# Second-level products for M7 and a new order of M6 and M7 in the last pass of a fused linear-attention and SwiGLU kernel

## The chip, the cores and the metric

The kernel runs on one core of one Trainium2 chip. The metric is the device time of one execution in microseconds. Three runs of the kernel before gave 756.44 us in the median (755.99 to 761.65). The profile is one more execution of the same program, recorded by the hardware profiler.

Names of engines as in the profile: PE is TensorE (matmuls), PEld its weight loads, DVE is VectorE, ACT is ScalarE, POOL is GpSimd, SP is SyncE, which here only issues DMAs. An engine name with a q (SPq, POOLq) is the engine's sequencer.

## The reference

The input is a sequence of 2048 rows of 1024 in bfloat16. What is computed, cut to the part that matters:

```python
def reference(A_x, A_wqkv, A_wo, B_x, B_w_gate, B_w_up, B_w_down):
    x = A_x
    xn = _layernorm(x, axis=-1)
    s = _A_ref(xn, A_wqkv, A_wo)          # linear attention, 32 heads of 32
    g = _silu(_B_ref(xn, B_w_gate, B_w_up, B_w_down))
    return x + s * g

def _B_ref(x, w_gate, w_up, w_down):      # w_gate, w_up: 1024 x 3584, w_down: 3584 x 1024
    g = _silu(x @ w_gate)
    u = x @ w_up
    return (g * u) @ w_down
```

## The kernel before

**Stages.** The first third of the time computes the attention part and stores `s` in DRAM. Then come two passes over 1024 tokens each, and each pass has two stages: a loop of 28 iterations (14 groups of gate columns and 14 of up columns, "keys") that makes the hidden activations `h`, and a down stage that multiplies `h` by `w_down`, applies silu, multiplies by `s` and adds `x`. The change touches the last pass alone: its loop (lines 1693 to 1744) and its down stage, `emit_down_m` (line 1394).

**Seven products in place of eight.** All large products use the scheme of Strassen and Winograd: a matrix product is cut into 2 x 2 quadrants and made of seven half-size products of sums of quadrants, so TensorE does 7/8 of the work and the other engines make the sums. In `emit_down_m` the seven are called M1 to M7. With `A` the activations, the operands on their side are A11 for M1, A12 for M2, A22 for M4 and the sums S1 = A21 + A22 (for M5), S2 = S1 - A11 (M6), S3 = A11 - A21 (M7) and S4 = A12 - S2 (M3). S1, S2 and S4 are written over A21, A11 and A12; S3 has two buffers of its own (`s3_`). The same sums of the weights are made in advance, in the first pass or earlier, and lie in DRAM (`wd_drams`).

**The second level.** The products listed in `L2` (M1, M2 and M4) are cut once more: `l2_M` (line 1469) makes each of seven quarter-size products, numbered 1 to 7 and taken in the order of `L2_ORDER`, 1, 2, 5, 6, 7, 4, 3. Each is made for two row halves r by `l2_p`, seven matmuls of 256 columns for each half. A product that is not in `L2` is made by `prod_t` in four tiles t of 128 rows, 14 matmuls of 512 columns each. The second level needs sums on both sides:

- of the weights: `l2_load` (line 1102) loads two blocks of a packed weight into a slot, `l2_sums` (line 1134) makes four differences on POOL and issues the store of the seven operands to DRAM on POOL's queue. One such load, sum and store is called a unit. M1 and M4 have four units each, in the loop of the last pass; M2's are made in the first pass.
- of the activations: `l2_lhs` (line 1160) makes four sums for one of seven blocks j on POOL, into the buffers of `l2_bufs`: for M1 two weight slots (`r_spare`), for M2 and M4 two tiles left from the first pass (`x_spare`, "kept" in the profile).

**Weight slots.** `w_slot` gives a tile from a pool of eight. Weights come through `load_w` in the order of `w_seq`; `load_w_to(n)` asks for all up to the n-th. In the loop iteration i calls `load_w_to(base + i + 5)`, from 17 on `+ 6`. Staged units take their slots from the same pool, and from iterations 17 and 18 on two more are set apart for `r_spare`. In the down stage `load(M, q)` asks for weights six or eight ahead; a product at the second level has four loads (three of 896 KB and one of 448), another has two halves of four DMAs each (line 260).

**Order of the work.** A manual schedule (line 382) keeps PE, DVE, ACT and POOL in the order of the program text. SP is not in it here: its order is made by the framework's planner, and like every queue it then runs in that order, so that a DMA that waits holds those behind it.

**One second-level product.** `l2_M` has two pairs of PSUM banks, `xw` and `zy`, each bank in two halves of 256 columns (`lo`, `hi`). Products 1 and 2 go to xw lo, 5 and 3 to xw hi, 6 to zy hi, 7 and 4 to zy lo; ACT copies between them, and the results are taken out by ACT (M1) or DVE additions, which all go through the helper `tt` (line 1418). For M1, whose results go straight to `KA`, these lines stand ahead of product 3, which writes `xw` hi again:

```python
for r in range(2):
    c0, c1 = c[r]
    ...
    tt(c1[:, hi], xw[r][:, hi], c1[:, hi])
fill()
```

`fill` inserts work for PE: in M1 the first two products of M2, in M2 the first tile of the next M. `banks` hands out two sets of four PSUM banks in turn. `sums` makes S1, S2 or S4 in seven operations of 1024 elements. `fins` and `flush` hold and run the final steps (`fin`, line 1196): two DVE operations (lines 1200, 1201), an out DMA and `io_load`, the load of the next x and s rows into one of five buffers.

Of the kernel before, what the change touches and what calls it, by code (L numbers as in the profile page):

```python
# [10 lines left out]
ALU = mybir.AluOpType  # L11
# [10 lines left out]
def kernel(  # L22
# [11 lines left out]
    nc = tc.nc  # L34
# [30 lines left out]
    NPK = 8  # L65
# [121 lines left out]
    NPASS = NB // 2  # L187
    passes = list(range(NPASS - 1, -1, -1))
    NWA = NFG // 2
    M_ORDER = (1, 2, 7, 6, 5, 4, 3)  # L190
    L2 = (1, 2, 4)
    L2_ORDER = (1, 2, 5, 6, 7, 4, 3)
    NQ = NFG // 2
    CH = CW // 2
    l2_drams = {}
# [756 lines left out]
    with ExitStack() as p3:  # L952
# [145 lines left out]

        l2_q = deque((M, j) for M in L2 if M != 2 for j in range(0, NQ, 2))
        l2_live = deque()  # L1100

        def l2_load():
            M, j0 = l2_q.popleft()
            kd, q = M_PACK[M]
            t = w_slot()
            v = t[:].rearrange("p h a b -> p (h a b)").rearrange("p (b j n) -> p b j n", b=8, n=CH)
            js = range(j0, min(j0 + 2, NQ))
            for j in js:
                for k, b0, b1 in ((0, 0, 7), (1, 1, 6)):
                    src = wd_drams[j][0 if kd == "a" else 1][:, k, q].rearrange("p (c n) -> p c n", n=CH)  # L1110
                    nc.sync.dma_start(out=v[:, b0:b1 + 1:b1 - b0, j - j0, :], in_=src)
            l2_live.append((M, js, v))
# [34 lines left out]
        x_spare, r_spare = [], []  # L1147

        def l2_bufs(M):
            v = [x[:].rearrange("p a b -> p (a b)").bitcast(F16) for x in x_spare]  # L1150
            if M == 1:
# [4 lines left out]
        def l2_quad(A, j):  # L1156
            v = A[:, :, j].rearrange("p k (r t n) -> p k r t n", r=2, t=2)
            return v[:, 0, :, 0], v[:, 1, :, 0], v[:, 0, :, 1], v[:, 1, :, 1]

        def l2_lhs(M, A, j, eng):  # L1160
            a11, a12, a21, a22 = l2_quad(A, j)
# [13 lines left out]
        for p in passes:  # L1175
# [4 lines left out]
            for hf in (1, 0):  # L1180
                for t in (2 * hf, 2 * hf + 1):
                    fq += [(p, t + TPB, 0), (p, t, 1), (p, t, 0)]

        def io_load(after=None):
            if not fq:
                return
            p, t, cc = key = fq.pop(0)
            r0 = p * TB2 + t * P
            pool, tg = (sp, "S%d" % len(fq)) if len(fq) < 3 else (iop, "io")
            io = pool.tile([P, 2, CW], BF16, name="io", tag=tg)  # L1190
            gate([nc.sync.dma_start(out=io[:, 0, :], in_=x2[r0:r0 + P, cc * CW:(cc + 1) * CW]),
                  nc.sync.dma_start(out=io[:, 1, :], in_=s_dram[r0:r0 + P, cc * CW:(cc + 1) * CW])],
                 after, sync=True)
            io_tiles[key] = io
# [199 lines left out]
        def emit_down_m(p, h, base):  # L1394
# [8 lines left out]
            def load(M, q=None):  # L1403

                n_ = max(i for i, key in enumerate(seq) if key[2][0] == M and q in (None, key[2][1])) + 1
                load_w_to(base + n_ + (NPK - 2 if M == 1 and q != 3 else NPK))

            def S3(k):
                return s3_[k // NWA][:, k % NWA]

            def lhs_of(M):
                if M == 7:
                    return S3
                v = {1: A11, 2: A12, 3: S4, 4: A22, 5: S1, 6: S2}[M]
                return lambda k: v[:, k]

# [52 lines left out]
            def l2_M(M, A, K, done, fill, in_place, dst=None):  # L1469
# [17 lines left out]
                load(M, 1)  # L1487
                for r in range(2):
                    l2_p(M, 7, r, A, bk)
                if K is None:  # L1490
# [19 lines left out]
                for r in range(2):  # L1510
                    c0, c1 = c[r]
                    if K is None:
                        nc.scalar.copy(out=c1[:, lo], in_=zy[r][:, lo])
                    else:
                        tt(c1[:, lo], zy[r][:, lo], K[2 * r + 1][:, lo])
                        done(2 * r + 1, c1)
                    l2_p(M, 3, r, A, bk)
                    if in_place:
# [17 lines left out]

            load_w_to(base + NPK - 2)
            KA = kept("kA")
            fins = deque()
            M7, M6, M5 = [], [], []  # L1540
            KB = []

            def fill7():
                M7.extend(banks())
                KB.extend(kept("kB"))
                prod_t(7, 0, M7[0], True)

            def done2(t, c):
                fins.append((t, 0, silu(c, "g11")))
            m2 = l2_M(2, quads(h, 1, 0), KA, done2, fill7, False)  # L1550
            for k in range(NFG):
                tt(S3(k), A11[:, k], A21[:, k], ALU.subtract)
            go(l2_M(1, quads(h, 0, 0), None, None, lambda: next(m2), False, KA))
            sums(S1, A21, A22, ALU.add)
            go(m2)
            sums(S2, S1, A11, ALU.subtract)
            for t in range(TPB):
                if t:
                    prod_t(7, t, M7[t], True)
                tt(KB[t], M7[t], KA[t])  # L1560
                flush(1)
            load(7)
            sums(S4, A12, S2, ALU.subtract)
            for j in range(NQ):
                l2_lhs(4, quads(h, 1, 1), j, nc.gpsimd)
            M6 = banks()
            for t in range(TPB):
                prod_t(6, t, M6[t], True)
                tt(KB[t], M6[t], KB[t])
                tt(KA[t], M6[t], KA[t])  # L1570
# [43 lines left out]
        for pi, p in enumerate(passes):  # L1614
# [78 lines left out]
            for i in range(n):  # L1693
                if first:
                    load_w_to(base + i + (na0 if i < n - 7 else 8 if i > n - 6 else 7))
                else:
                    load_w_to(base + i + (5 if i < 17 else 6))
                if i + 1 < n:
                    emit_a(keys[i + 1])
                    emit_c22(keys[i + 1])  # L1700
# [31 lines left out]
                if not first:  # L1732
                    if l2_live:
                        l2_sums()
                    if i in (17, 18):
                        r_spare.append(w_slot())
                    if i % 2 == 1 and l2_q:
                        l2_load()
                    if i >= 18 and 4 * l2_j + 4 <= i:
                        l2_lhs(1, quads(h, 0, 0), l2_j, nc.gpsimd)  # L1740
                        l2_lhs(2, quads(h, 1, 0), l2_j, nc.gpsimd)
                        l2_j += 1
                if deferred:
                    deferred.pop(0)()
            base += n
            if last_pass:
                l2_lhs(2, quads(h, 1, 0), NQ - 1, nc.gpsimd)
# [36 lines left out]
```

## Time and profile before

| | us |
|---|---|
| median of three runs (lowest, highest) | 756.44 (755.99, 761.65) |
| the profiled execution | 756.18 |
| its span, first to last instruction | 754.4 |
| the last pass: loop, down stage | 499 to 669, 669 to 754 |

Granted TensorE clock: 0.999 of full speed. Times in the trace count from the start of the span. A group line of the page gives line, engine, operation, output and input tiles, shape and count, then busy time, mean of one in ns, and idle time of the engine just before. Matmul lengths are modelled and overlap: 512 columns appear as 379 ns each, while in the stream they start 216 ns apart.

Busy time by engine in some stretches of the last pass (columns: stretch, its length, then PE, PEld, DVE, ACT and POOL busy with counts, clock, share of the DMA engines, GB/s):

```profile
539.00:560.00 21.00, 21.00 (x99) 9.47 (x97) 14.36 (x17) 7.08 (x10) 6.14 (x7) 1.00 0.80 274
640.00:667.00 27.00, 27.00 (x127) 12.26 (x126) 19.32 (x23) 7.78 (x11) 9.38 (x14) 1.00 0.46 151
690.00:700.00 10.00, 10.00 (x62) 5.87 (x60) 9.13 (x16) 2.67 (x4) 7.05 (x8) 1.00 1.06 379
710.00:720.00 10.00, 10.00 (x48) 4.58 (x47) 10.00 (x13) 0.00 (x0) 5.39 (x6) 1.00 0.81 259
```

The operand sums on POOL and the loads of whole product weights:

```profile
L1166 POOL TENSOR_TENSOR kept<-hT,kept 128x256 f16<-128x256 bf16 x8 | 7.5, 934 | 5.2 <-PE dm L1466 5.2
w_sb<-wd SPq DMA_DIRECT2D x24, 256.0 KB, 5.5
```

### The profile page before, as it was taken

Reading aid. Unit: us, or ns where it says so; the run is one execution under the profiler, and the core shown is the slowest. Engines: PE = TensorE matmul, PEld = TensorE weight load, DVE = VectorE, ACT = ScalarE, POOL = GpSimd, SP = SyncE. Lnnn points to the kernel's source line nnn. Section 1 sums busy time; section 2 is a strip of 40 time slices with the busy share of each in tenths; the row PEclk is TensorE's granted clock in tenths of the full one; section 3 lists DMA queues with packets and bytes.
Section 4 is the critical chain, followed back from the end, with each engine's and each line's share of the span. In section 5 each row is a group of like instructions: output and inputs, shape, how many; then the busy total and the mean of one; then the engine's idle time right before and its main releaser. Section 6 shows DMA issues by size and latency. Waiting matters only on the chain.

```text
span 754.4 us, 11075 instructions
## 1 busy us (share of the span) xinstructions
PE 745.8 (99%) x3857; PEld 360.8 (48%) x3857; DVE 581.4 (77%) x1040; ACT 381.1 (51%) x545; POOL 399.8 (53%) x500
## 2 busy tenths in 40 slices
PE   8999999999999999999999999999999999999997
PEld 3544444454454444444444444444444444467464
DVE  6687787887697788888889785468776877687966
ACT  5677776889956575656658311132323222232023
POOL 2444799998540266868585021811542569434900
PEclk9999999999999999999999999999999999999999
DMA  9967799879779668878799228789786768479652
GB/s 318 304 146 139 228 332 298 303 158 271 206 190 296 231 214 301 295 279 316 273 323 409 111 65 306 222 295 339 258 306 222 281 206 344 147 258 318 209 161 77
DMA packets 129160, 187.77 MB, mean 249 GB/s; under 512 B 36208, under 2 KB 104176, under 8 KB 119376
## 3 DMA queue, kind: packets, MB, share of 16 engines
q1 hardware_dynamic: 121760, 156.00, 63.9%
q0 software_dynamic: 5904, 28.58, 9.9%
q10 hardware_dynamic: 1440, 2.49, 1.1%
q8 instruction: 30, 0.49, 0.3%
q14 instruction: 26, 0.21, 0.1%
HBM read 119.47 MB, written 60.23 MB: 238 GB/s over the span
## 4 chain that ended last, share of the span: by engine, by line
PE 84%; DMA 7%; POOL 3%; DVE 2%; issue 2%; ACT 1%; SPq 1%; POOLq 0%; DVEq 0%; ACTq 0%
PE zw L966 19%; PE kv_ps L554 15%; PE xb L966 10%; PE q_ps L183 6%; PE dzw L1228 6%; PE dm L1430 6%; PE yb L966 5%; PE dm L1466 4%; PE dx L1228 3%; DMA l<-w_sb 3%; PE fx L816 3%; DMA w_sb<-wd 3%; PE s_ps L774 3%; POOL w_sb L1144 2%; PE dy L1228 2%
## 5 line engine op out<-in xcount | busy, mean ns | idle before, releaser
L966 PEld LDWEIGHTS <-w_sb 128*128 128x128 f16 (+1 forms) x1568 | 152.1, 98 | 183.8 <-DMA w_sb<-pk_u 1.3
L966 PE MATMUL xb<-xnT,w_sb 128*128 128x512 bf16 x448 | 115.0, 379 | 0.0
L554 PE MATMUL kv_ps<-wkv_sb,xnT 128*128 128x512 bf16 x512 | 113.7, 379 | 0.6 <-ACT xnT L543 0.4
L966 PE MATMUL zw<-xnT,w_sb 128*128 128x512 bf16 x448 | 105.8, 379 | 0.0
L966 PE MATMUL zw<-S,w_sb 128*128 128x512 f16 x448 | 105.8, 379 | 0.0
L321 POOL TENSOR_TENSOR w_sb<-w_sb 128x512 f16<-128x512 bf16 x42 | 50.2, 1195 | 95.7 <-DVE w_sb L309 51.3
L286 ACT ACTIVATE w_sb<-w_sb 128x2048 bf16<-128x2048 bf16 x42 | 79.9, 1902 | 3.9 <-DMA w_sb<-in_B_w_up_dram 3.9
L554 PEld LDWEIGHTS <-xnT 128*128 128x128 bf16 x512 | 48.3, 97 | 56.0 <-ACT xnT L543 0.8
L1144 POOL TENSOR_TENSOR w_sb<-w_sb 128x512 f16<-128x512 bf16 (+3 forms) x32 | 35.4, 1126 | 52.4 <-DMA w_sb<-wd 51.9
L1042 ACT ACTIVATE sg<-cg 128x1024 bf16<-128x1024 f32 x28 | 29.6, 1057 | 57.4 <-DVE cg L1035 57.4
L183 PE MATMUL q_ps<-xnT,wq_sb 128*128 128x512 bf16 x256 | 58.4, 379 | 0.0
L966 PE MATMUL yb<-S,w_sb 128*128 128x512 f16 x224 | 57.4, 379 | 0.8 <-DMA w_sb<-pk_u 0.8
L1035 DVE SCALAR_TENSOR_TENSOR cg<-zw,rc_all,s 128x1024 f32<-128x1024 f32 x28 | 35.9, 1284 | 25.3 <-PE zw L966 13.2
L994 DVE SCALAR_TENSOR_TENSOR s<-yb,rc_all,s 128x512 f32<-128x512 f32 x42 | 31.5, 749 | 27.3 <-ACT s L993 27.3
L322 POOL TENSOR_TENSOR w_sb<-w_sb 128x512 f16<-128x512 bf16 x42 | 50.5, 1202 | 3.3
L324 POOL TENSOR_TENSOR w_sb<-w_sb 128x512 f16<-128x512 bf16 x42 | 50.3, 1197 | 0.0
L323 POOL TENSOR_TENSOR w_sb<-w_sb 128x512 f16<-128x512 bf16 x42 | 50.2, 1196 | 0.0
L1202 POOL DMA_DIRECT2D out_dram<-io x16 | 8.9, 555 | 69.2 <-DVE io L1201 69.0
L993 ACT ACTIVATE s<-xb,rcl 128x512 f32<-128x512 f32 x14 | 9.6, 687 | 66.3 <-PE xb L966 66.3
L1228 PE MATMUL dx<-w_sb,hT 128*128 128x512 bf16 x112 | 42.4, 379 | 0.0
L993 ACT ACTIVATE s<-xb,rc_all 128x512 f32<-128x512 f32 x42 | 28.4, 676 | 22.0 <-issue 12.7
L309 DVE TENSOR_SCALAR w_sb<-w_sb,cs_all 128x2048 bf16<-128x2048 bf16 x35 | 36.7, 1048 | 2.8
(213 smaller groups left out, 1351.1 us busy)
## 6 DMA issues: line engine op xcount, KB each, us to landing
w_sb<-pk_g SPq DMA_DIRECT2D x27, 1024.0 KB, 6.6
pk_g<-w_sb SPq DMA_DIRECT2D x14, 1024.0 KB, 5.0
w_sb<-pk_u SPq DMA_DIRECT2D x14, 1024.0 KB, 8.3
pk_u<-w_sb POOLq DMA_DIRECT2D x13, 1024.0 KB, 5.8
w_sb<-l SPq DMA_DIRECT2D x9, 896.0 KB, 4.6
w_sb<-in_B_w_gate_dram SPq DMA_DIRECT2D x14, 512.0 KB, 6.4
w_sb<-in_B_w_down_dram SPq DMA_DIRECT2D x28, 256.0 KB, 4.8
w_sb<-in_B_w_up_dram SPq DMA_DIRECT2D x14, 512.0 KB, 5.4
```

Source lines behind the costliest of these rows:

```text
L183: nc.tensor.matmul(q_ps[:], lhsT=wq_sb[:, dc, g * P:(g + 1) * P], rhs=xn_ap(dc, btok), start=(dc == 0), stop=(dc == DC - 1))
L286: nc.scalar.activation(out=junk, in_=raw_view(key, t), func=ACT.Square, accum_out=asum[:])
L321: nc.gpsimd.tensor_tensor(out=T1, in0=b12, in1=b11, op=ALU.subtract)
L322: nc.gpsimd.tensor_tensor(out=T2, in0=b22, in1=T1, op=ALU.subtract)
L323: nc.gpsimd.tensor_tensor(out=T3, in0=b22, in1=b12, op=ALU.subtract)
L324: nc.gpsimd.tensor_tensor(out=T4, in0=b21, in1=T2, op=ALU.subtract)
L554: mm = nc.tensor.matmul(kv_ps[:], lhsT=xn_ap(dc, tok), rhs=wkv_sb[:, dc, c * CW:(c + 1) * CW], start=(dc == 0), stop=(dc == DC - 1))
L966: mm = nc.tensor.matmul(out, lhsT=lhs(k), rhs=rhs(k), start=(first and k == 0), stop=(k == HK - 1), skip_group_check=True)
L993: nc.scalar.activation(out=s1[:], in_=x_[:], func=ACT.Copy, scale=rc)
L1144: nc.gpsimd.tensor_tensor(out=b(o_), in0=b(a_), in1=b(b_), op=ALU.subtract)
L1228: nc.tensor.matmul(out, lhsT=lhs, rhs=rhs, start=first, stop=lastk, skip_group_check=True)
L1430: nc.tensor.matmul(out, lhsT=lhs_of(M)(k)[:, t * P:(t + 1) * P], rhs=w_of(M, k)[:, cols], start=first and k == 0, stop=k == NFG - 1, skip_ ...
```

## The change

M7 joins `L2`. The order becomes M1, M2, M6, M7, M5, M4, M3: M6's first tile is now what fills the gap in M2, M5's first tile fills the gap in M7. S1 is made ahead of M1, S2 between M1 and the rest of M2. S3 is made in eight operations instead of 14. The four operand sums of M7 and of M4 are made by `l2_lhs_r`, on DVE, for a row half at a time (seven blocks of 128 in one operation), between the additions of M6 and of M5; for M4 they replace `l2_lhs` on POOL. `r_spare` is taken once, at the first unit, and its two slots serve in turn for all units (now 12), then for M1's operand sums and last for M7's; until M7 ends the down stage asks for weights only six ahead. POOL makes M1's sums from iteration 22 on, two blocks j an iteration, and M2's in every fourth iteration. In the loop of the last pass SP too is kept in the order of the program, with `io_load` put off by three iterations.

```diff
-    M_ORDER = (1, 2, 7, 6, 5, 4, 3)
-    L2 = (1, 2, 4)
+    M_ORDER = (1, 2, 6, 7, 5, 4, 3)
+    L2 = (1, 2, 4, 7)
+    L2_FROM = 22
+    L2_UNITS = (3, 4, 6, 7, 9, 10, 12, 13, 15, 16, 18, 19)
...
+        x_spare, r_spare = [], []
         def l2_load():
             M, j0 = l2_q.popleft()
             kd, q = M_PACK[M]
-            t = w_slot()
+            while len(r_spare) < 2:
+                r_spare.append(w_slot())
+            t = r_spare[len(l2_q) % 2]
...
+        def l2_lhs_r(M, A, r, eng):
+            if not isinstance(A, tuple):
+                A = (A[:, 0], A[:, 1])
+            v = [a.rearrange("p j (r t n) -> p j r t n", r=2, t=2)[:, :, r] for a in A]
+            a11, a12, a21, a22 = v[0][:, :, 0], v[1][:, :, 0], v[0][:, :, 1], v[1][:, :, 1]
+            s1, s2, s3, s4 = [x[:, :, r] for x in l2_bufs(M)]
+            eng.tensor_tensor(out=s1, in0=a21, in1=a22, op=ALU.add)
+            eng.tensor_tensor(out=s2, in0=s1, in1=a11, op=ALU.subtract)
+            eng.tensor_tensor(out=s3, in0=a11, in1=a21, op=ALU.subtract)
+            eng.tensor_tensor(out=s4, in0=a12, in1=s2, op=ALU.subtract)
...
         def io_load(after=None):
             if not fq:
                 return
+            if hold[0] and after is None:
+                io_due.append(hold[0])
+                return
...
-                load_w_to(base + n_ + (NPK - 2 if M == 1 and q != 3 else NPK))
+                load_w_to(base + n_ + (NPK - 2 if M in (1, 2, 6, 7) and (M, q) != (7, 3) else NPK))
...
-            m2 = l2_M(2, quads(h, 1, 0), KA, done2, fill7, False)
-            for k in range(NFG):
-                tt(S3(k), A11[:, k], A21[:, k], ALU.subtract)
+            m2 = l2_M(2, quads(h, 1, 0), KA, done2, fill6, False)
+            for j0, j1 in ((0, 2), (2, 4), (4, 6), (6, 7)):
+                for k in range(2):
+                    tt(S3[k][:, j0:j1], A11k[:, k, j0:j1], A21k[:, k, j0:j1], ALU.subtract)
+            sums(S1, A21, A22, ALU.add)
             go(l2_M(1, quads(h, 0, 0), None, None, lambda: next(m2), False, KA))
-            sums(S1, A21, A22, ALU.add)
+            sums(S2, S1, A11, ALU.subtract)
             go(m2)
-            sums(S2, S1, A11, ALU.subtract)
             for t in range(TPB):
                 if t:
-                    prod_t(7, t, M7[t], True)
-                tt(KB[t], M7[t], KA[t])
-                flush(1)
-            load(7)
+                    prod_t(6, t, M6[t], True)
+                if t in (0, 1):
+                    l2_lhs_r(7, S3, t, nc.vector)
+                tt(KA[t], M6[t], KA[t])
+                if t > 1:
+                    flush(2)
+            load(6)
             sums(S4, A12, S2, ALU.subtract)
-            for j in range(NQ):
-                l2_lhs(4, quads(h, 1, 1), j, nc.gpsimd)
-            M6 = banks()
+            KB = kept("kB")
+            go(l2_M(7, S3, KA, None, fill5, False, KB))
             for t in range(TPB):
-                prod_t(6, t, M6[t], True)
-                tt(KB[t], M6[t], KB[t])
-                tt(KA[t], M6[t], KA[t])
-            load(6)
-            M5 = banks()
-            for t in range(TPB):
-                prod_t(5, t, M5[t], True)
+                if t:
+                    prod_t(5, t, M5[t], True)
                 c = k2([P, CW], FP32, "c22")[:]
                 tt(c, M5[t], KB[t])
+                if t in (0, 1):
+                    l2_lhs_r(4, quads(h, 1, 1), t, nc.vector)
                 fins.append((t + TPB, 1, silu(c, "g22")))
-                if len(fins) > 1:
+                if t > 1:
                     flush(1)
...
+            sp_man = ExitStack()
+            if last_pass:
+                sp_man.enter_context(tc.manual_schedule(engines={mybir.EngineType.SP}))
...
-                    load_w_to(base + i + (5 if i < 17 else 6))
+                    load_w_to(base + i + (5 if i < L2_FROM else 6))
+                    hold[0] = False
+                    while io_due and io_due[0] <= i:
+                        io_due.popleft()
+                        io_load()
+                    hold[0] = i + 3
...
-                    if i in (17, 18):
-                        r_spare.append(w_slot())
-                    if i % 2 == 1 and l2_q:
+                    if l2_q and i in L2_UNITS:
                         l2_load()
-                    if i >= 18 and 4 * l2_j + 4 <= i:
-                        l2_lhs(1, quads(h, 0, 0), l2_j, nc.gpsimd)
-                        l2_lhs(2, quads(h, 1, 0), l2_j, nc.gpsimd)
-                        l2_j += 1
+                    for _ in range(2):
+                        if i >= L2_FROM and 4 * l2_j + 4 <= i:
+                            l2_lhs(1, quads(h, 0, 0), l2_j, nc.gpsimd)
+                            l2_j += 1
+                    if i % 4 == 0 and i >= 4:
+                        l2_lhs(2, quads(h, 1, 0), i // 4 - 1, nc.gpsimd)
```

More of the change, by code (lines that the diff above doesn't have):

```diff
@@ L1145, in l2_sums @@
             nc.gpsimd.dma_start(out=l2_drams[M][:, :, js.start:js.stop, :], in_=v[:, 0:7, 0:n_, :])
-        x_spare, r_spare = [], []
         def l2_bufs(M):
             v = [x[:].rearrange("p a b -> p (a b)").bitcast(F16) for x in x_spare]
-            if M == 1:
+            if M in (1, 7):
                 v = [x[:].rearrange("p h a b -> p (h a b)").bitcast(F16) for x in r_spare]
@@ L1156, in l2_quad @@
         def l2_quad(A, j):
+            if isinstance(A, tuple):
+                v = [a[:, j].rearrange("p (r t n) -> p r t n", r=2, t=2) for a in A]
+                return v[0][:, :, 0], v[1][:, :, 0], v[0][:, :, 1], v[1][:, :, 1]
             v = A[:, :, j].rearrange("p k (r t n) -> p k r t n", r=2, t=2)
             return v[:, 0, :, 0], v[:, 1, :, 0], v[:, 0, :, 1], v[:, 1, :, 1]
+        def l2_lhs_r(M, A, r, eng):
[8 more added lines that the diff above has]
+            eng.tensor_tensor(out=s4, in0=a12, in1=s2, op=ALU.subtract)
         def l2_lhs(M, A, j, eng):
@@ L1182 @@
                     fq += [(p, t + TPB, 0), (p, t, 1), (p, t, 0)]
+        io_due = deque()
+        hold = [False]
         def io_load(after=None):
             if not fq:
+                return
+            if hold[0] and after is None:
+                io_due.append(hold[0])
                 return
@@ L1405, in load @@
                 n_ = max(i for i, key in enumerate(seq) if key[2][0] == M and q in (None, key[2][1])) + 1
-                load_w_to(base + n_ + (NPK - 2 if M == 1 and q != 3 else NPK))
-            def S3(k):
-                return s3_[k // NWA][:, k % NWA]
+                load_w_to(base + n_ + (NPK - 2 if M in (1, 2, 6, 7) and (M, q) != (7, 3) else NPK))
             def lhs_of(M):
-                if M == 7:
-                    return S3
                 v = {1: A11, 2: A12, 3: S4, 4: A22, 5: S1, 6: S2}[M]
@@ L1489, in l2_M @@
                     l2_p(M, 7, r, A, bk)
-                if K is None:
+                if dst is not None:
                     c = [dst[0:2], dst[2:4]]
@@ L1515, in l2_M @@
                         tt(c1[:, lo], zy[r][:, lo], K[2 * r + 1][:, lo])
+                    if done is not None:
                         done(2 * r + 1, c1)
@@ L1538, in emit_down_m, with fill6, fill5 @@
             KA = kept("kA")
[L1539 to L1546, printed above, removed]
+            M6, M5 = [], []
+            def fill6():
+                M6.extend(banks())
+                prod_t(6, 0, M6[0], True)
+            def fill5():
+                M5.extend(banks())
+                prod_t(5, 0, M5[0], True)
             def done2(t, c):
@@ L1549, in done2 @@
                 fins.append((t, 0, silu(c, "g11")))
-            m2 = l2_M(2, quads(h, 1, 0), KA, done2, fill7, False)
-            for k in range(NFG):
-                tt(S3(k), A11[:, k], A21[:, k], ALU.subtract)
+            S3 = tuple(x[:] for x in s3_)
+            m2 = l2_M(2, quads(h, 1, 0), KA, done2, fill6, False)
+            A11k, A21k = [v.rearrange("p (j k) t -> p k j t", k=2) for v in (A11, A21)]
+            for j0, j1 in ((0, 2), (2, 4), (4, 6), (6, 7)):
+                for k in range(2):
+                    tt(S3[k][:, j0:j1], A11k[:, k, j0:j1], A21k[:, k, j0:j1], ALU.subtract)
@@ L1734 @@
                         l2_sums()
-                    if i in (17, 18):
-                        r_spare.append(w_slot())
-                    if i % 2 == 1 and l2_q:
+                    if l2_q and i in L2_UNITS:
                         l2_load()
-                    if i >= 18 and 4 * l2_j + 4 <= i:
-                        l2_lhs(1, quads(h, 0, 0), l2_j, nc.gpsimd)
-                        l2_lhs(2, quads(h, 1, 0), l2_j, nc.gpsimd)
-                        l2_j += 1
+                    for _ in range(2):
[4 more added lines that the diff above has]
+                        l2_lhs(2, quads(h, 1, 0), i // 4 - 1, nc.gpsimd)
                 if deferred:
                     deferred.pop(0)()
+            hold[0] = False
+            while io_due:
+                io_due.popleft()
+                io_load()
+            sp_man.close()
             base += n
```

## The prediction

> **What bounds the kernel now.** I read the page first, then the list of waits, then the timelines of PE, DVE and SP in the last pass, which is all that the change touches. The page says who is the bound, and the list of PE's waits says that nothing stands ahead of it:
>
> ```profile
> span 754.4 us, 11075 instructions
> PE 745.8 (99%) x3857; PEld 360.8 (48%) x3857; DVE 581.4 (77%) x1040; ACT 381.1 (51%) x545; POOL 399.8 (53%) x500
> ```
>
> ```profile
> PE warm_ps L590 <- DVE warm L587: 1.5, 1, 1.5
> PE yb L966 <- DMA w_sb<-pk_u: 0.8, 1, 0.8
> ```
>
> PE idles 0.8 us in the last pass for a weight, 0.3 us on ACT in M4, and not otherwise. So only two things can change the time: PE's own work, and new waits of PE. The chain of waits, which leaves PE at 539 us and goes through staged units, their stores and POOL until 623.8 us, ends in just that 0.8 us. The timeline of PE gives the second price:
>
> ```profile
> 621.11 1.89 PE L966 MATMUL zw<-xnT,w_sb 128*128 128x512 bf16 x8
> 623.81 1.04 PE L966 MATMUL yb<-S,w_sb 128*128 128x512 f16 x4 [0.82 <-DMA w_sb<-pk_u]
> ...
> 680.95 1.69 PE L1466 MATMUL dm<-w_sb 128*128 128x256 bf16 x14
> 682.47 4.75 PE L1466 MATMUL dm<-w_sb,kept 128*128 128x256 f16 x42
> 687.06 3.19 PE L1430 MATMUL dm<-w_sb,S3h 128*128 128x512 f16 x14
> 690.08 1.69 PE L1466 MATMUL dm<-w_sb,hT 128*128 128x256 f16 x14
> 691.61 1.69 PE L1466 MATMUL dm<-w_sb,kept 128*128 128x256 bf16 x14
> 693.14 9.23 PE L1430 MATMUL dm<-w_sb,S3h 128*128 128x512 f16 x42
> 702.20 24.34 PE L1430 MATMUL dm<-w_sb,hT 128*128 128x512 f16 x112
> ```
>
> Columns: start, length, engine, line, operation, tiles, shape, count. Lengths overlap, so I take differences of starts. The line at 680.95 is product 3 of M1; M7 is at 687.06 and at 693.14. VectorE in the same stretch:
>
> ```profile
> 671.18 7.15 DVE L1418 TENSOR_TENSOR S3h<-hT 128x512 f16<-128x512 bf16 x14
> 678.25 0.74 DVE L1418 TENSOR_TENSOR kA<-dm,kA 128x256 f32<-128x256 f32 x2
> 681.91 0.42 DVE L1418 TENSOR_TENSOR kA<-dm,kA 128x256 f32<-128x256 f32 x1 [2.92 <-PE dm L1466]
> 682.67 0.42 DVE L1418 TENSOR_TENSOR kA<-dm,kA 128x256 f32<-128x256 f32 x1 [0.34 <-PE dm L1466]
> 683.02 5.71 DVE L1418 TENSOR_TENSOR hT<-hT 128x1024 f16<-128x1024 bf16 x7
> ```
>
> **M7 at the second level.** Removed: 12.08 us of PE (687.06 to 690.08, 693.14 to 702.20: 56 matmuls of 512 columns, 0.216 us each). Added: 98 matmuls of 256 columns. M1 and M2 are 196 such and take 18.34 + 3.06 us (668.72 to 687.06, 690.08 to 693.14), so M7 takes 10.70. PE saves **1.38 us**. [...]
>
> **Staging in two slots of its own.** In the loop of the last pass the weight that PE waited for was issued at 618.67 us, 8.7 us after the one before it in SP's queue, and landed 5.1 us later. From the last start before it (621.11 + 1.89 - 0.38 = 622.62) plus 0.216 to 623.81 PE lost 0.97 us (0.38 is one matmul's length). After the change weights no longer share slots with staging. In a ring of six, iteration i asks for key i+4, which takes key i-2's slot, free when iteration i-2 ends; PE needs it when iteration i+3 begins. That is four iterations of 28 matmuls, 6.05 us each: 24.2 us, less 7.3 us of landing (median of these loads; 17.6 at most, in the burst at the pass's start) leaves 16.9 us of slack. I take the **0.97 us** as gone. Four more units (M7) add 16 POOL subtractions of about 1.2 us and four stores of 0.9 us of issue to POOL, 23 us, in a loop of 169 us where POOL is half idle; nobody on PE waits for them. VectorE's loop share is about 75%, and PE never waits for it there.
>
> **Order of VectorE's work.** Here the change adds a wait. S1 is now queued ahead of M1, so S3 and S1 both stand before the two additions that read xw's upper half (678.25 now). Product 3 of M1 overwrites that half and has to wait for them; its start is 680.95, so today they are 2.3 us early. With POOL's last eight operand sums running, S3's operations of 512 start 0.81 us apart, after them 0.335 (five of 0.885 us until 675.2, nine of 0.415 after); operations of 1024 start 1.075 apart with POOL (seven of hT from 693.7 take 7.4), 0.60 without (first three of the line at 683.02). S3 in eight operations: five beside POOL, 5 x 1.075, one of 0.60, two of 0.335: 6.65, ending at 677.83. S1: 7 x 0.60 = 4.2, ending at 682.03. The first addition ends at 682.45. PE waits from 680.95: **1.50 us**. Bounds: 0 if S1 is hidden after all, and 4.8 if POOL is beside S1 all along (7 x 1.075). I take the uncontended row since POOL's last operation of this stage ends at 675.0.
>
> [...]
>
> S2 follows M1's last addition (683.02 + 1.50 = 684.5) and ends at 688.7. M6's first tile starts at 687.06 + 1.50 = 688.6 and needs the last two of S2's 14 blocks 12 matmuls later, at 691.1: hidden, cover 2.4 us; without it, with POOL beside S2, it ends at 692.0 and costs 0.9. The sums for M7 and M4 are 16 operations of 896 elements on VectorE, about 0.53 us each between the rows of 512 and 1024: 8.5 us. They lie where POOL's 28 sums for M4 fell away, and with them the contention: S2 and S4 go from 7.4 and 7.1 to 4.2 each, eight operations of the final steps from about 0.85 to 0.42. VectorE gains as much as it takes on. S4 ends near 710.2, M7's evacuation is due at 711.4. The tail after M4 is unchanged.
>
> **Slots of the ring in the down stage.** Until M7 is through there are six, not eight. M6's halves take the slots of M2's first and M1's third block (free at 679.4 and 681.0), as the loads issued at 679.6 and 682.0 do today, and are due from 688.6: fine. M5 is the tight one: its loads wait for M6's end.
>
> ```profile
> 675.43 17.21 SPq L260 DMA_DIRECT2D w_sb<-wd  x24
> ...
> 708.43 1.50 SPq L1202 DMA_DIRECT2D out_dram<-io  x2
> 709.99 0.42 SPq L253 DMA_DIRECT2D w_sb<-l  x1
> 713.38 0.34 SPq L1191 DMA_DIRECT2D io<-in_A_x_dram  x1
> ```
>
> Today M5's eight loads are within the first line, ten microseconds early. After: M6's slots fall free at 702.2 and 703.75; eight loads take 10.7 us from first issue to last landing (M3's, first issued at 715.24, last at 719.8 with the median 6.1 to land). Issued behind two stores at 703.1 they are complete at 713.8, and the last block is due at 714.0. It just fits; I take 0, bounds 0 and 4 (the 3.4 us for which SP stood between 709.99 and 713.38, and 0.6 of issue).
>
> **Sum.** -1.38 - 0.97 + 1.50 = -0.85. The profiled execution took 756.18 us (span 754.4), so 755.33; the median of the runs shown is 0.26 above that execution: **755.6 us**.
>
> **The rivals.**
> - *No wait at product 3.* If the wait falls away (S1 runs faster, or the additions get ahead), all of 2.35 us stays: 754.1. Against it: the order on VectorE is the program's. Chance 0.12.
> - *M5's weights are late.* SP's order is the planner's: today a block for M4 whose slot was free earlier stands behind two stores, and four more loads behind their landing. If half of M5 stands behind those, PE waits 1 to 4 us before M5's second half: 756.6 to 759.6, middle 758.1. Chance 0.25.
> - *POOL is late and runs beside S1 and S2.* 24 sums for M1 now start only at iteration 22, 16 us of work in the 33 us to the loop's end. If they slip past it, product 3 waits 4.8 us and M6's first tile another 1.0 (S2 from 687.9 to 695.4, due at 694.4): 759.9. It is the pairing of operations again, 1.075 against 0.60; the cover is some 15 us, so chance 0.06.
> - *SP becomes the bound in the loop* (slower). In program order a unit's load that waits for its slot's store holds every weight behind it. Today SP waited 47.0 us in 5 such waits, 9.4 each:
>
> ```profile
> SPq L1111 <- DMA l<-w_sb: 47.0, 5, 10.1
> SPq L263 <- DMA l<-w_sb: 22.3, 3, 9.1
> ```
>
>  Ten of the 12 units reuse a slot, two per three iterations. At 9.4 each, with 3.8 of issue for the units and 1.2 for three weights, that is 23.8 us per 18.15: five groups fall back 28 us, less 16.9 of slack is 11 us on PE: 766.7. It decides from a mean wait of about 8.3 us. Against it: a slot's turn is 2.7 (load) + 4.9 (sums) + 4.7 (store) and 2.6 for other sums on POOL, 14.9 in 18.15 us, so the waits should be 2 to 5. Chance 0.06.
> - *The change doesn't do what it says*: the 0.97 us comes back elsewhere in the loop: 756.6. Chance 0.06.
>
> **How the numbers follow.** Forecast 0.45, rivals 0.12, 0.25, 0.06, 0.06, 0.06. The range goes from 753.7 (the first rival, less the 0.4 us between the lower two runs) to 759.7 (the top of the second); about 0.12 lies outside. 1% is 7.6 us, about what a measurement of this kernel can tell from no change. Faster than 748.9 would need three times all gains: 0.01. Slower than 764.0: the SP case and a heap of the others: 0.07. Within: 0.92.
>
> **What would show it.** Right: 56 matmuls at line 1430 fewer and 98 of 256 columns more; no wait of yb for pk_u; one new wait of PE, about 1.5 us, at M1's product 3 on an addition of VectorE at the helper line 1418; hT sums of 0.68 us, none of 1.15. Wrong: PE waiting for w_sb<-wd before M5 (the second rival), for pk weights (SP), or for hT sums before M6 (POOL). If PE's 12.08 us did not become about 10.7, the first term falls.

## Result and profile after

The changed kernel takes **764.05 us** in the median (763.46 to 766.53, six runs), beside 756.53 us for the kernel before, run at the same time (755.99 to 761.65, six runs): a ratio of 1.0094, 95% interval 1.0073 to 1.0116. The profiled execution took 763.46 us. So the change costs some 7 us, where 0.8 us of gain was forecast. The head of the page, and the list of PE's waits, of the changed kernel:

```profile
span 761.7 us, 11138 instructions
...
PE 744.1 (98%) x3835; PEld 365.7 (48%) x3899; DVE 579.7 (76%) x1054; ACT 382.7 (50%) x549; POOL 395.6 (52%) x492
```

```profile
PE dm L1448 <- DMA w_sb<-wd: 3.8, 1, 3.8
...
PE dm L1484 <- DVE kA L1436: 1.4, 1, 1.4
```

PE has less to do, and two new waits. (Its weight loads, 3899 in place of 3857, show the 98 - 56 = 42 matmuls more; 64 of the matmuls' own records are missing from this trace. Lines moved: the helper `tt` is now 1436, matmuls of first-level products 1448, of second-level ones 1484; SP's loads of weight halves 262, of packed pieces 255, of staged units 1116; outs 1225, x and s loads 1214 and 1215.) Where the 7.3 us of span went, by starts of matmuls, with the two kernels' last pass cut at its first matmul, the first `dm` matmul and the last matmul:

| us | before | after | difference |
|---|---|---|---|
| all ahead of the last pass | 498.51 | 499.12 | +0.61 |
| loop of the last pass | 170.20 | 169.43 | -0.77 |
| down stage | 80.86 | 87.97 | +7.11 |
| from the last matmul's start to the end | 4.82 | 5.17 | +0.35 |

The first row lies ahead of all that was changed, and moves from one execution to the next (498.4 to 499.3 in the profiles below). The down stage is the matter. Its PE timeline, from M1's product 3 on (start, length, engine, line, operation, tiles, shape, count, and in brackets the idle time before and its releaser):

```profile
682.36 1.69 PE L1484 MATMUL dm<-w_sb 128*128 128x256 bf16 x14 [1.41 <-DVE kA L1436]
...
703.61 3.22 PE L1484 MATMUL dm<-w_sb,S3h 128*128 128x256 f16 x28
706.67 4.75 PE L1484 MATMUL dm<-w_sb 128*128 128x256 f16 x42
711.25 1.97 PE L1448 MATMUL dm<-w_sb,hT 128*128 128x512 f16 x7
717.01 3.45 PE L1448 MATMUL dm<-w_sb,hT 128*128 128x512 f16 x7 [3.79 <-DMA w_sb<-wd]
720.25 2.64 PE L1484 MATMUL dm<-w_sb,S3h 128*128 128x256 f16 x14
722.73 1.69 PE L1484 MATMUL dm<-w_sb 128*128 128x256 f16 x14
724.26 9.23 PE L1448 MATMUL dm<-w_sb,hT 128*128 128x512 f16 x42
```

M7's first five products take 703.61 to 711.25, as counted. Then M5's first tile makes seven matmuls, stands, and goes on at 717.01; and what follows is too long: seven matmuls of 512 take 720.25 - 717.01 = 3.24 us in place of 7 x 0.216 = 1.51, the next 14 of 256 take 2.48 us and only the 14 after them the usual 1.53. The stretches of that time say why (stretch, length, busy time and count of PE, PEld, DVE, ACT, POOL, granted clock, DMA share, GB/s):

```profile
711.00:713.00 2.00, 1.87 (x11) 0.90 (x10) 2.00 (x7) 0.00 (x0) 0.00 (x0) 1.00 0.74 220
713.00:715.00 2.00, 0.22 (x2) 0.00 (x0) 0.50 (x2) 0.00 (x0) 0.00 (x0) 1.00 0.80 225
715.00:717.00 2.00, 0.00 (x0) 0.00 (x0) 0.00 (x0) 0.00 (x0) 0.00 (x0) 0.59 0.81 244
717.00:719.00 2.00, 1.84 (x5) 0.54 (x5) 0.00 (x0) 0.00 (x0) 0.00 (x0) 0.50 0.92 293
719.00:721.00 2.00, 2.00 (x8) 0.99 (x7) 0.00 (x0) 0.00 (x0) 0.00 (x0) 0.50 0.92 362
721.00:723.00 2.00, 2.00 (x15) 1.55 (x14) 0.42 (x1) 0.00 (x0) 0.00 (x0) 0.71 1.02 412
```

The granted clock fell to 0.50 while PE stood, and stayed there until about 722.2. From M5's first matmul to its second tile 13.01 us pass; 14 x 0.216 and 28 x 0.109 are 6.08. The excess of 6.93 is 4.25 of waiting (0.30 in a short stop at 712.1, 3.95 in the long one) and 2.68 of matmuls at half clock: 7.25 from 717.01 to 724.26, in place of 1.51 + 3.06. With 1.57 at product 3 (682.36, in place of 680.79) and M7's -1.38 this makes 7.12, the whole of the down stage's +7.11.

And this is why the weights came late, SP's timeline:

```profile
702.36 0.34 SPq L1225 DMA_DIRECT2D out_dram<-io  x1
702.79 0.53 SPq L262 DMA_DIRECT2D w_sb<-wd  x1
703.41 0.55 SPq L1225 DMA_DIRECT2D out_dram<-io  x1
704.01 0.53 SPq L262 DMA_DIRECT2D w_sb<-wd  x1
704.63 0.59 SPq L1214 DMA_DIRECT2D io<-in_A_x_dram  x1
...
708.55 1.21 SPq L262 DMA_DIRECT2D w_sb<-wd  x2
710.77 0.34 SPq L1214 DMA_DIRECT2D io<-in_A_x_dram  x1
...
712.58 2.31 SPq L262 DMA_DIRECT2D w_sb<-wd  x4
```

M5's eight loads leave in four lots (one, one, two and four), between four outs and eight loads of x and s. The second half's four go out from 712.58, half a microsecond before PE needs the first of them; that one landed at 716.97, the last at 719.11.

VectorE's timeline, finally, against the prediction's working for S3 (671.02), S1 (677.68) and the first additions:

```profile
671.02 6.73 DVE L1436 TENSOR_TENSOR S3h<-hT 128x1024 f16<-128x1024 bf16 x8
677.68 4.29 DVE L1436 TENSOR_TENSOR hT<-hT 128x1024 f16<-128x1024 bf16 x7
681.89 0.74 DVE L1436 TENSOR_TENSOR kA<-dm,kA 128x256 f32<-128x256 f32 x2
```

S3 takes 6.66 from start to start (6.65 worked out), S1 4.21 (4.2), and product 3 follows the additions, 1.57 us late (1.50).

### The profile page after: what moved, and what is told of

It is laid out like the page before. It is cut to its first block, busy times and chain, and to the rows that moved or that the text cites. A ratio compares the mean times of both kernels' runs of the same rounds, so it can differ in the third digit from the quotient of the medians.

```text
span 761.7 us, 11138 instructions
## 1 busy us (share of the span) xinstructions
PE 744.1 (98%) x3835; PEld 365.7 (48%) x3899; DVE 579.7 (76%) x1054; ACT 382.7 (50%) x549; POOL 395.6 (52%) x492
## 4 chain that ended last, share of the span: by engine, by line
PE 91%; DVE 4%; DMA 2%; issue 1%; ACT 1%; SPq 1%; DVEq 0%; ACTq 0%
PE zw L968 25%; PE kv_ps L556 14%; PE xb L968 13%; PE yb L968 6%; PE q_ps L183 6%; PE dzw L1251 6%; PE dm L1484 4%; PE dx L1251 3%; PE fx L818 3%; PE dm L1448 3%; PE s_ps L776 2%; PE dy L1251 2%; PE kvz L578 1%; PE nd L745 1%; DMA wkv_sb<-in_A_wqkv_dram 1%
## 5 line engine op out<-in xcount | busy, mean ns | idle before, releaser
L968 PE MATMUL xb<-xnT,w_sb 128*128 128x512 bf16 x420 | 113.3, 379 | 1.5
L1149 POOL TENSOR_TENSOR w_sb<-w_sb 128x512 f16<-128x512 f16 (+3 forms) x48 | 50.9, 1082 | 28.9 <-DMA w_sb<-wd 28.1
L1448 PE MATMUL dm<-w_sb,hT 128*128 128x512 f16 (+3 forms) x180 | 39.1, 372 | 4.2 <-DMA w_sb<-wd 3.8
```

The lines of the kernel that those rows point to most:

```text
L968: mm = nc.tensor.matmul(out, lhsT=lhs(k), rhs=rhs(k), start=(first and k == 0), stop=(k == HK - 1), skip_group_check=True)
L1448: nc.tensor.matmul(out, lhsT=lhs_of(M)(k)[:, t * P:(t + 1) * P], rhs=w_of(M, k)[:, cols], start=first and k == 0, stop=k == NFG - 1, skip_ ...
```

## The experiments

Theory after this result: two independent waits, S1's place on VectorE (1.57 us) and M5's weights behind other DMAs in SP's order (4.25 us), and the second carries a third cost, the clock (2.68 us). Rivals: the ring of six slots is the limit whatever the order; the clock fell for another reason; the wait at product 3 is absorbed later. All numbers of the experiments first (profiled execution in the last four columns; ratio to the kernel before run beside it, 757.5 us in the median in the first four rows and 757.65 in the next four):

| kernel | median (lowest, highest) us | ratio, 95% interval | span | loop | down stage | end |
|---|---|---|---|---|---|---|
| late S1 | 762.64 (760.92, 764.24) | 1.0067, 1.0045 to 1.0089 | 760.62 | 169.21 | 87.52 | 5.16 |
| busy gap | 762.80 (761.86, 763.76) | 1.0069, 1.0049 to 1.0090 | 761.14 | 169.21 | 87.57 | 5.18 |
| eight slots | 756.05 (755.78, 756.51) | 0.9980, 0.9970 to 0.9990 | 754.03 | 169.21 | 81.04 | 5.17 |
| M5's loads first | 756.49 (754.88, 757.36) | 0.9978, 0.9963 to 0.9993 | 754.74 | 169.94 | 81.03 | 5.17 |
| late S1 + eight slots | 754.53 (754.04, 756.44) | 0.9956, 0.9939 to 0.9974 | 754.57 | 170.65 | 79.47 | 5.18 |
| late S1 + loads first | 754.36 (753.89, 757.30) | 0.9956, 0.9939 to 0.9974 | 752.81 | 169.46 | 79.63 | 5.16 |
| late S1 + eight slots, M7 at the first level | 755.19 (755.02, 755.79) | 0.9966, 0.9948 to 0.9983 | 753.25 | 169.21 | 80.86 | 4.80 |
| late S1 + eight slots, SP's order in the loop left free | 755.15 (754.34, 756.63) | 0.9968, 0.9951 to 0.9985 | 752.94 | 169.92 | 79.47 | 5.17 |

**Late S1.** S1's sums go into M1's fill, behind M1's additions:

```diff
-            sums(S1, A21, A22, ALU.add)
-            go(l2_M(1, quads(h, 0, 0), None, None, lambda: next(m2), False, KA))
+            def fill1():
+                sums(S1, A21, A22, ALU.add)
+                next(m2)
+            go(l2_M(1, quads(h, 0, 0), None, None, fill1, False, KA))
```

> S1 is moved into M1's fill, behind the two additions that product 3 waits for. Theory (each new wait of PE is paid in full): the 1.4 us wait of dm for DVE kA is gone, M6's first tile still finds S2 ready, and the time falls by 1.5 us, from 764.0 to 762.5. Rival (the wait is absorbed by the later wait for M5's weights, whose landing time is set by other things): the wait is gone, the wait for w_sb<-wd grows by as much, and the time stays at 764.0.

The wait at product 3 is gone, so its cause is shown. What that is worth is not shown here. The median is 1.4 us below the changed kernel's, as the theory has it, but the two were not run beside each other; the down stage of the profiled execution is only 0.45 us shorter. PE stops for 0.30 us in M6's first tile, at 688.7, reaches M5 1.28 us earlier in the stage, and waits there for the same loads (its PE timeline; a fourth stop, of 0.22, follows):

```profile
710.81 0.81 PE L1448 MATMUL dm<-w_sb,hT 128*128 128x512 f16 x3 [0.43 <-DMA w_sb<-wd]
714.35 0.38 PE L1448 MATMUL dm<-w_sb,hT 128*128 128x512 f16 x1 [2.73 <-DMA w_sb<-wd]
715.57 1.87 PE L1448 MATMUL dm<-w_sb,hT 128*128 128x512 f16 x4 [0.84 <-DMA w_sb<-wd]
```

From M5's first matmul to its second tile 13.83 us pass here, 13.01 in the changed kernel, and 14.49 in the changed kernel profiled again (below). A stretch that differs by 1.48 us between two executions of one program can't tell from one profile whether 1.57 us are paid or absorbed. The reason that the rival gave is not borne out: the loads do move with PE, and the last four went out 1.16 us earlier in the stage.

**Busy gap.** Sixteen more matmuls of 512 columns into a bank that is started afresh later, between the halves of M5's first tile:

```diff
-                prod_t(5, 0, M5[0], True)
+                for k in range(NWA):
+                    mm(5, 0, k, M5[0], True)
+                for k in range(16):
+                    nc.tensor.matmul(M5[1], lhsT=lhs_of(5)(k % NWA)[:, 0:P], rhs=w_of(5, k % NWA), start=True,
+                                     stop=True, skip_group_check=True)
+                for k in range(NWA, NFG):
+                    mm(5, 0, k, M5[0], True)
```

> 16 matmuls that compute nothing of use (into the bank of M5's second tile, which is started anew afterwards) are put between the two halves of M5's first tile, 3.5 us in the 4.2 us in which PE waits there. Theory (the granted clock falls because PE stands still, and the slow matmuls behind the wait are a price of their own): M5's second half still starts at the same time, the granted clock stays at 1.0 between 715 and 723 us, and the time falls by 2.7 us, to 761.3. Rival (the matmuls behind the wait are slow for want of data): they stay slow, and the time stays at 764.0 or rises by up to 3.5 us.

A stretch of this kernel, columns as above (the clock is 1.00 in the next two us as well):

```profile
715.00:717.00 2.00, 2.00 (x10) 0.78 (x8) 0.00 (x0) 0.00 (x0) 0.00 (x0) 1.00 0.88 255
```

The clock stays at 1.00, and the 14 matmuls of M7's product 4 take 1.53 us again (2.48 in the changed kernel). So here it was PE's standing that took the clock: the longest stop left at M5 is 1.08 us, in place of 3.79. The time itself moved less than the 2.68 us. SP issued the same DMAs in the same order, the last four weights from 712.57 (712.58 in the changed kernel), but the first of these landed at 718.04, and M5's second half started at 718.08, 1.07 us later than in the changed kernel. Such landings differ between executions (716.06 in the changed kernel profiled again), so the size of the clock's part rests on the changed kernel's own rows.

**Eight slots.** M7's operand sums go into `x_spare`, as M2's and M4's do, so the ring has eight slots in the down stage:

```diff
-            if M in (1, 7):
+            if M == 1:
...
-                load_w_to(base + n_ + (NPK - 2 if M in (1, 2, 6, 7) and (M, q) != (7, 3) else NPK))
+                load_w_to(base + n_ + (NPK - 2 if M == 1 and q != 3 else NPK))
```

> M7's operand sums go into the tiles that M2's used (kept), so the two staging slots fall free after M1, and the down stage asks for weights eight ahead again. Theory (M5's loads are late because their slots are those of M6): all loads of M5 are issued before 700 us, PE does not wait for w_sb<-wd, the clock does not fall, and the time falls by 4.2 + 2.7 = 6.9 us, to 757.1. Rival (the DMA engines cannot bring M6, M7 and M5 in time whatever the slots): a wait of over 1 us for a weight stays somewhere in M6, M7 or M5, and the time stays above 760.

**M5's loads first.** The slots stay six. The loads are asked for ahead of the last addition of M6, and the outs with their x and s loads come after the loop:

```diff
-                tt(KA[t], M6[t], KA[t])
-                if t > 1:
-                    flush(2)
-            load(6)
+                if t == TPB - 1:
+                    load(6)
+                tt(KA[t], M6[t], KA[t])
+            flush(4)
```

> Still six slots, but M5's loads stand ahead of the four final steps of M2 in the program, so that SP issues all eight of them before those steps' four stores and eight loads of x and s. Theory (SP's order makes the loads late, not the slots alone): the eight are issued from 702.2 to 707.5, the last lands by 713, PE waits under 1 us, too little for the clock to fall, and the time falls by 6 to 6.9 us, to 757 to 758. Rival (the slots alone, and 10.7 us for eight loads): the last lands at 714 or later, PE waits 1 to 2.5 us, and the time falls by 3 us or less if the clock still falls.

Both take the whole of M5's 6.93 us away (down stage 81.04 and 81.03, from 87.97), the clock stays at 1.0, and both kernels are now a little below the kernel before. With six slots and the loads first, SP issues all eight of M5 in a row and then, from 707.23, the four outs (its timeline); the last of the eight landed at 712.44:

```profile
702.27 4.85 SPq L262 DMA_DIRECT2D w_sb<-wd  x8
```

So the number of slots was not the limit: more of them hid SP's order, and the order alone was enough.

In the kernel with eight slots the list of PE's waits names another releaser for the 1.4 us at product 3:

```profile
PE dm L1484 <- DMA w_sb<-wd: 1.4, 1, 1.4
```

Place and size are those of the wait that the changed kernel's list puts down to VectorE, and VectorE's first addition ends just ahead of product 3 as there (681.57 and 681.61; 682.31 and 682.36 in the changed kernel). This had to be told apart, by the next kernel.

**Late S1 and eight slots together.**

> The changed kernel with two edits at once: S1's sums inside M1's fill (behind M1's additions on VectorE) and M7's operand sums in x_spare, so that the ring has eight slots again and loads are asked for eight ahead except in M1. Theory (the wait at M1's product 3 is the queue on VectorE): the starts 1.68 us apart at about 680 us in the kernel with eight slots come back to about 0.11, M5 does not wait for weights, and the down stage falls from 81.0 to about 79.5 us; time 756.05 - 1.5 = 754.5 us, about 2 us below the kernel before. Rival A (the list of waits is right to name the weight there): the 1.4 us at product 3 stay, 756.0. Rival B (absorbed): the gap goes, but S2, queued later, holds M6 or the last additions, and the down stage stays at 81: 756.0.

The stop at 680 us is gone, though nothing was done about weights there; the name in the list was wrong, VectorE was the cause. The down stage fell from 81.04 to 79.47, all of the 1.57 us, which the first experiment could not show; profiled again (below), it is 79.47 once more. Its PE timeline at M5 and M7:

```profile
703.41 3.22 PE L1484 MATMUL dm<-w_sb,S3h 128*128 128x256 f16 x28
...
711.05 3.19 PE L1448 MATMUL dm<-w_sb,hT 128*128 128x512 f16 x14
714.07 1.69 PE L1484 MATMUL dm<-w_sb,S3h 128*128 128x256 f16 x14
...
717.13 9.23 PE L1448 MATMUL dm<-w_sb,hT 128*128 128x512 f16 x42
```

**Late S1 and M5's loads first, six slots.**

> S1's sums inside M1's fill, six slots as the change has them, and M5's weights asked for ahead of the stores and of the x and s loads. Theory (order of SP, not the number of slots, is what M5 needs): no wait of PE before M5, clock 1.00 through, no gap at 680 us; 756.49 - 1.5 = 755.0, within 0.5 us of the kernel with eight slots and late S1. Rival (six slots are too few once PE is 1.5 us earlier): PE waits for w_sb<-wd again before M5, some 1 to 2 us, 756 to 757.

No wait of PE at M5, and the same time as with eight slots; SP issues the eight loads from 700.34 to 705.2, then the four outs. The down stage is 0.16 us longer, by a stop of 0.16 in M6's first tile at 688.7, where late S1 alone has 0.30.

**M7 at the first level again**, on top of late S1 and eight slots:

```diff
-    L2 = (1, 2, 4, 7)
+    L2 = (1, 2, 4)
...
-            go(l2_M(7, S3, KA, None, fill5, False, KB))
+            M7 = banks()
+            for t in range(TPB):
+                prod_t(7, t, M7[t], True)
+                tt(KB[t], M7[t], KA[t])
+            load(7)
+            fill5()
```

> Late S1 and eight slots as in the first of these kernels, with M7 at the first level again: 56 matmuls of 512 columns for M7, no units and no operand sums for it, M5's first tile behind M7. Theory (M7's second level saves PE 12.08 - 10.70 = 1.38 us, nothing else on the path): 1.4 us above the first kernel, some 755.9. Rival A (what M7's units and sums cost in the loop and on VectorE eats it): the same time as the first kernel within 0.4 us. Rival B (it costs more than it saves): below the first kernel by 0.5 us or more.

PE's timeline at M7 and at the start of M5 (the line of first-level matmuls is 1450 here):

```profile
701.08 12.25 PE L1450 MATMUL dm<-w_sb,S3h 128*128 128x512 f16 x56
713.16 12.25 PE L1450 MATMUL dm<-w_sb,hT 128*128 128x512 f16 x56
```

M7 takes 12.08 us here, and 711.05 - 703.41 + 717.13 - 714.07 = 10.70 in the kernel above: the 1.38 of the prediction to the digit, and 1.39 in the down stage. The medians differ by 0.66 only. The end of the kernel, from the last matmul on, is 4.80 us here, as in the kernel before, and 5.16 to 5.18 in every kernel with M7 at the second level; so 0.37 of the gain is given back there, after all work of PE. The traces show where. At the program's end SP goes through a row of short waits, 0.06 us each. In every kernel with M7 at the second level six of them come after the one for the last out (in the kernel above that out landed at 753.28 and SP's last wait began at 753.67); here and in the kernel before none does (752.34 and 752.36 here). What orders these waits was not tried. The other 0.35 is not traced; the twelve runs of the two kernels range over 2.4 and 0.8 us.

**SP's order in the loop left to the planner**, and with it the loads of x and s no longer put off, again on late S1 and eight slots:

```diff
-            if last_pass:
+            if False:
                 sp_man.enter_context(tc.manual_schedule(engines={mybir.EngineType.SP}))
...
-                    hold[0] = i + 3
```

> Late S1 and eight slots as in the first of these kernels, but SP's order in the last pass's loop made by the planner again and the loads of x and s not put off. Theory (the 0.97 us of the kernel before came from staging sharing slots with weights): PE does not wait in the loop, last-pass loop 169.4 us, the same time as the first kernel within 0.4 us. Rival (it came from the planner's order of SP): PE waits 0.5 us or more for a weight in the loop, loop 170.2 us, some 1 us more in all.

There is a wait in the loop after all, 0.91 us between starts at 568.1 us, and the loop is 169.92. But the kernel with SP in program order had strays in that profile too, and a longer loop. So four kernels were profiled once more without any change (one execution each: 757.34, 765.05, 754.24 and 758.73 us):

> The kernel before, unaltered, profiled once more. Theory (its 0.97 us stall in the last pass's loop is a fixed part of it, from staging in the weights' slots): starts 1.20 us apart at about 622.6 us again, loop 170.2 us. Rival (a stray wait of that one execution): another place, or none, loop 169.2 to 171.

> The changed kernel, unaltered, profiled once more. Theory (SP's order is fixed in the program): the 4.2 us between starts in M5's first tile and the clock of 0.50 behind it come again, down stage 87.5 to 88.5 us, and the loop is 169.2 to 169.5 us without a stall. Rival (chance of that execution): the stop before M5 differs by over 1 us.

> The kernel with late S1 and eight slots, profiled once more. Theory (the loop has no fixed stall; the 1.4 us above 169.2 in its first profile were strays): loop 169.2 us, span 753.1, down stage 79.5. Rival (the staging loop has a fixed stall): starts 0.7 and 1.1 us apart at about 508 and 529 us again, loop 170.6.

> Late S1, eight slots and the planner's order of SP in the loop, profiled once more. Theory (the wait for pk_g at 568 us is a fixed part of the planner's order): starts 0.9 us apart at about 568 us again, loop 169.9. Rival (a stray): loop 169.2, or a wait elsewhere.

The kernel before stalls at the same weight again, longer, loop 171.02; its PE timeline:

```profile
624.99 1.04 PE L966 MATMUL yb<-S,w_sb 128*128 128x512 f16 x4 [1.48 <-DMA w_sb<-pk_u]
```

The kernel with late S1 and eight slots has no stall this time (loop 169.21, span 752.46): its former ones, at 508 and 529 us, were strays. The place at 508 us, in the burst of loads at the pass's start, has a wait for `pk_g` in three of the ten profiles with SP in program order, 0.24 to 0.69 us. With the planner's order the wait at 568 us is there again and three times as long (loop 173.66). PE stands 2.58 us, and the clock falls after it (PE's timeline, then stretches with columns as above):

```profile
571.30 1.16 PE L968 MATMUL yb<-S,w_sb 128*128 128x512 f16 x4 [2.58 <-DMA w_sb<-pk_g]
```

```profile
573.00:575.00 2.00, 1.89 (x5) 0.76 (x5) 0.07 (x1) 0.69 (x1) 1.70 (x3) 0.50 0.93 344
575.50:576.00 0.50, 0.50 (x3) 0.20 (x2) 0.18 (x1) 0.00 (x0) 0.27 (x1) 1.00 1.03 401
```

Of the 4.45 us above 169.21, 2.74 are the wait, by starts, and 1.71 the matmuls at half clock. The cause of the wait in SP's timeline, in that execution:

```profile
554.74 11.10 SPq L1116 DMA_DIRECT2D w_sb<-wd  x6
565.93 0.42 SPq L265 DMA_DIRECT2D w_sb<-pk_g  x1
```

Six loads of staged units, four of one and two of the next, stand ahead of the weight `pk_g`, and ahead of the fifth SP waits 7.0 us (557.96 to 564.97) for the store that empties its slot. The weight landed at 571.25; PE started on it at 571.30. In program order the same weight (in both executions 15 loads of `pk` weights follow it) goes out 18.7 us earlier, ahead of these units (SP's timeline of the kernel with late S1 and eight slots, profiled again):

```profile
547.23 0.45 SPq L265 DMA_DIRECT2D w_sb<-pk_g  x1
550.59 0.33 SPq L265 DMA_DIRECT2D w_sb<-pk_u  x1
562.29 1.91 SPq L1116 DMA_DIRECT2D w_sb<-wd  x4
```

There SP waits as well, 11 us ahead of 562.29, and PE does not. So the theory that slots of its own alone free the loop fell: the stall moved from `pk_u` at 623 to `pk_g` at 568, and went with slots and program order together. Program order without slots of its own was not run, so whether order alone would do is open.

The changed kernel, profiled again, waits before M5 as expected, but in four pieces and for longer (5.2 us in all, the longest 2.2), with the clock at 0.50 again; its down stage is 89.45, one microsecond above the range expected, and its loop had one stray at 508 us. Place and cause are fixed, the size is not: it depends on when each load lands.

## Why the prediction was wrong

The time lay above its range, on the slower side; slower than 764.0 had 0.07. Put in, what was measured closes the sum for the profiled execution: 755.33 + 6.93 (M5) + 0.07 (product 3) + 0.20 (staging) + 0.35 (the end) + 0.61 (ahead of the pass) = 763.49, against 763.46.

- *The step that failed: "It just fits; I take 0, bounds 0 and 4", of M5's weight loads.* The sum took the eight loads as issued one behind the other from 703.1, 10.7 us to the last landing. The order is the planner's, as the second rival said, and it put four x and s loads and two outs behind the second of the eight, and four more x and s loads ahead of the last four. The last landed at 719.11 in place of 713.8. Issued in a row, in the kernel with M5's loads first, the eight took 10.2 us (702.27 to 712.44): the length was right, the place in the queue was not. The second rival came true, at the top of what it gave and past it: 4.25 us of wait where it had 1 to 4. It had a chance of 0.25 against 0.45, and the rows shown spoke for it: in the kernel before SP stands between 709.99 and 713.38 in front of such loads. What was weighed wrongly is that today's cover of ten microseconds hid this, and the change spends just that cover.
- *A term that was missing: the clock.* 2.68 us of matmuls at half clock, behind the wait. The kernel before does show it, at its end, in stretches that the prediction does not show. PE's last matmul starts at 749.58, and the granted clock, 1.00 up to 752, falls before the span ends (last stretch, columns as above):

```profile
752.00:754.40 2.40, 0.00 (x0) 0.00 (x0) 0.00 (x0) 0.00 (x0) 0.00 (x0) 0.59 0.24 68
```

 The shortest single stop behind which the clock fell in these runs was 2.58 us; a price that the prediction gave to a wait as long as that should have had something on top. With 2.7 us the top of the second rival would have been 759.6 + 2.7 = 762.3, and the range with it.
- *M7 at the second level, -1.38:* right, 1.38 by M7's own rows in two kernels.
- *The wait at product 3, +1.50:* right, 1.57, with the place and the engine named. That the whole of it is VectorE's queue is shown by the kernel with late S1 and eight slots.
- *Staging, -0.97:* right in size (170.20 to 169.43; 169.21 in the profiles without a stray) and wrong in its reason. Slots of its own did not do it alone; SP's program order, which the prediction put among the dangers, had to be there too.
- *SP becomes the bound in the loop:* it did not. SP waits 7.9 us in each of 7 such waits (55.2 in all), close to the 8.3 from which that rival decides, but it counted on ten waits. PE waits in the loop for none of them.
- *Order of VectorE's other work:* right. S2 is out of the way of M6, the sums for M7 follow each other at 0.57 us (0.53 estimated), and S1, S2 and S4 go at 0.60 us an operation, as without POOL.
- *"The tail after M4 is unchanged":* wrong by 0.35, small; it lies in SP's last waits.

## What to carry to other kernels

With ten microseconds of cover M5's loads needed no thought about their place in a queue; a change that spends the cover has to read what the queue will hold at that time, in the order in which the queue is filled, and not when the slot is free. The clock fell here behind single stops of PE of 2.58 and 3.79 us, at a price of 1.71 and 2.68 us, and not behind one of 1.41: when a wait comes out as long as the first two, price the clock behind it as well. And mend the larger, unsteady wait first, or both at once: beside M5's wait, which differed by 1.48 us between two executions, the repair of 1.57 could not be read, and after that wait was gone it showed in full. Both together turned a loss of 0.9% into a gain of 0.4% (0.9956, 0.9939 to 0.9974).

## What the runs showed of the hardware

**In four executions the half clock lasted 3.41 or 6.83 us.** In finer stretches of the same place the clock fell at 715.35 and came back at 722.18 in the changed kernel, 715.05 and 721.88 with late S1, 717.38 and 724.21 in the changed kernel profiled again (each worked out from the mean clock of a half microsecond): 6.83 us each time. In the loop with the planner's order of SP, profiled again, it fell at 572.09 and came back at 575.50: 3.41 us. In all four the last 3.41 us before the clock came back hold no wait of PE for a weight or for another engine. In the loop PE was at work all the while, and the price was half the length: 1.71 us for the 3.41.

**In one execution the clock fell after the stop was over.** In that loop PE had been at work again for 0.79 us (from 571.30) when it fell, after a single stop of 2.58 us.

**One matmul between two stops did not keep the clock up.** With late S1 the longest idle time was 2.73 us and then 0.84, with one matmul of 0.38 between them; in the changed kernel profiled again it was 2.23 and 1.05 with one between (PE's timeline of that execution):

```profile
716.10 0.38 PE L1448 MATMUL dm<-w_sb,hT 128*128 128x512 f16 x1 [2.23 <-DMA w_sb<-wd]
717.53 1.87 PE L1448 MATMUL dm<-w_sb,hT 128*128 128x512 f16 x4 [1.05 <-DMA w_sb<-wd]
```

The clock fell both times, within the second idle time (at 715.05 and 717.38). A stop of 1.41 us between busy stretches, at product 3, left the clock at 1.00.
